# A linear-attention and gated-MLP block on one core: query blocks as seven products for eight, three PSUM banks a unit, and a computed order of the helpers

## The chip, the core and the metric

The kernel runs on one core of a Trainium2 chip. The core has five instruction queues that run at the same time and wait for each other by semaphores: TensorE (PE) for matmuls into PSUM, ScalarE (ACT), VectorE (DVE), GpSimd (POOL), and SyncE (SP), from which nearly all DMAs are issued here. PSUM is used as eight banks of 128 partitions by 512 float32. The metric is the device time of one execution in microseconds; it was run three times.

## The reference

```python
x = A_x                                   # [1, 2048, 640], bfloat16
xn = layernorm(x)                         # over the 640, eps 1e-5
q, k, v = split(xn @ wqkv)                # 32 heads of 20 columns each
phi = lambda t: where(t > 0, t + 1, exp(t)) + 1e-6
pq, pk = phi(q), phi(k)
kv = einsum("bhsd,bhse->bhde", pk, v)     # per head, 20 x 20
z = einsum("bhsd->bhd", pk)
num = einsum("bhqd,bhde->bhqe", pq, kv)
den = einsum("bhqd,bhd->bhq", pq, z)[..., None] + 1e-6
s = heads_to_columns(num / den) @ wo      # wo: [640, 640]
g = silu(relu(xn @ w1) @ w2)              # w1: [640, 1728], w2: [1728, 640]
return x + s * g
```

## The kernel before, in words

**Tiles.** The 2048 tokens are 16 tiles of 128 (`t`), or four chunks of 512 (`j`). The 640 columns are five blocks of 128 (`k`, `c`). The 1728 hidden columns are 13 blocks of 128 and one of 64 (`f`, 14 in all). Everything stays in SBUF after its load.

**The order of work.** A class `Sched` (L21) notes for each operation what it reads and writes, and puts in the semaphore waits that follow from it. It does not move anything: every engine executes its operations in the order in which the program text records them, so a helper on VectorE that stands early in the text and waits holds up all of VectorE's work recorded after it. The order is written out by hand, as lists of helpers beside each step of TensorE's work (L1100 to L1283 for the first half, L1560 to L1664 for the second).

**Stages.**
1. Layernorm statistics and normalisation of each tile (`bn` L467, `aggr` L472, `LN_norm` L497) on DVE, with the reciprocal root on POOL. The first four tiles are transposed by TensorE, the others by a transposing DMA on SP (`xnT_dma` L545).
2. Key tiles (`K_mm` L551): 10 matmuls of 320 columns into two banks, evacuated by ScalarE twice (`K_evac` L566: exp, relu, over both banks at once), and finished on DVE (`K_fin` L581) into `pk`. For tiles 8 to 11 one more matmul (`whole`, L562) writes the columns 320 to 511 of the first bank, so that a later instruction that adds to the whole bank finds it started.
3. Query blocks, transposed (`Q_mm` L607): for each chunk and each block of 128 columns, 5 matmuls of 512 columns, evacuated by ScalarE (exp, relu) and summed by DVE (`f_sum`) into `pqT`: 4 x 5 = 20 blocks.
4. Hidden blocks (`H_mm` L655, narrow block `H_half` L665), transposed, into `hT`. The tokens of the first chunk are not yet scaled when their hidden blocks of `HP` are made; `scale_rows` (L939) and `scale_bcast` (L942) bring the 512 row scales into every partition with four matmuls against the identity (L943) and a ScalarE copy, and `scale_h` (L948) multiplies them in.
5. The gram matrix `GT` of `xn` and `pk`, the sums `z` (`z_sum` L750, `z_col` L765), the denominators (`den` L782), their reciprocals on DVE (`den_rec` L794). SP stores the reciprocals to DRAM, each repeated for the 20 columns of its head (`den_store` L803), and loads them back in the layout of the queries (`load_recip` L811, one 640 KB transfer for a chunk each way). `divide` (L818) multiplies the queries by them on DVE.
6. `kv_group` (L1288) makes each head's 20 x 20 product from `GT`, masked by DVE, and `W_block` (L1317) its product with `wo`, so that the attention output is one product of the divided queries with the result, `wf`.
7. For pairs of tiles, `U_steps` (L1405) makes the gate (hidden times w2, evacuated with silu by `gate_q` L1352), and `O_steps` (L1477) the attention output, which DVE multiplies by the gate straight from PSUM (`s_out` L1540, `s_mult` L1515) and adds to x (`s_store` L1520), and SP stores, 160 KB a tile. The first pair of output tiles is made by plain tiles (`s_tile` L1535), the last pair too: `s_tile` of tile 14 and `s_last` (L1550), which takes tile 15 in three pieces of 224, 208 and 208 columns, with a product after each, the first piece added on POOL and stored on another queue.

**Seven products for eight.** Ten pairs of hidden blocks in the first half (`h_unit` L1002, two chunks of tokens by two blocks of columns), the gram matrix (`seven` L894), the gate and the middle output pairs use the Strassen-Winograd form: a 2 x 2 block product from seven products of sums and differences, which DVE prepares in SBUF (`h_S`, `h_T`, `g_S`, `g_T1` and so on, `u_S`, `u_T`, `o_S`, `o_T`). The 640 columns are split two blocks, two blocks, and a fifth that is left over and done plainly (`last`). A unit is seven steps, in the order s1, s5, s6, s2, s7, s3, s4, and takes four banks `bd`, `ba`, `bb`, `bc`:

```python
        def s7():
            mm(7, ba)
            cp(ps[bd], ("ps", bd), ba)
...
        def s4():
            mm(8, ba)
            dst = hT[:, i + 6, schunk(j1)]
            tt(dst, ps[ba], s5, ALU.add, [("ps", ba), skey], [("hT", j1, i + 6)])
...
            mm(4, bd)
```

That is: after product 1, ScalarE copies bank `ba` into `bb`, on which product 2 accumulates; product 5 goes to SBUF; after product 6, DVE adds `ba` and product 5 into `bc`, on which product 3 accumulates. After product 7 ScalarE copies `ba` into the fourth bank `bd`, on which product 4 accumulates, while `ba` takes product 8 (the left-over fifth block) and gives the fourth quarter.

Of the kernel before, what the change touches and what calls it, by code (L numbers as in the profile page):

```python
# [11 lines left out]
class _Res:  # L12
    __slots__ = ("w", "r", "nread")

    def __init__(self):
        self.w = None
        self.r = {}
        self.nread = 0


class Sched:  # L21

    def __init__(self, nc, n_dma_sems):
        self.nc = nc
        self.ops = {E: [] for E in ENGS}
        self.count = {E: 0 for E in CENGS}
        self.gseq = 0
        self.seq_at = {E: [] for E in CENGS}
        self.seq_at_dma = []
        self.vc = {E: {} for E in ENGS}  # L30
        self.vc_at = {E: [] for E in CENGS}
        self.vc_at_dma = []
        self.res = {}
        self.ndma = 0
        self.dma_sem_of = []
        self.dsem_count = [0] * n_dma_sems
        self.dsem_last_k = [None] * n_dma_sems
        self.n_dma_sems = n_dma_sems
        self.allow_unread = set()

# [18 lines left out]
    def _require(self, E, agents, waits):  # L59
        need_eng = {}  # L60
        need_dma = []
        for a in agents:
            if self._known(E, a):
                continue
            if a[0] == "D":
                if a not in need_dma:
                    need_dma.append(a)
            else:
                if need_eng.get(a[0], -1) < a[1]:
                    need_eng[a[0]] = a[1]  # L70
        items = [("E", Ep, idx, self.seq_at[Ep][idx]) for Ep, idx in need_eng.items()] + \
                [("D", a[1], None, self.seq_at_dma[a[1]]) for a in need_dma]
        items.sort(key=lambda x: -x[3])
        for kind, a1, a2, _sq in items:
            if kind == "E":
                Ep, idx = a1, a2
                if self._known(E, (Ep, idx)):
                    continue
                waits.append(("E", Ep, idx + 1))
                vc = self.vc[E]  # L80
                vc[Ep] = max(vc.get(Ep, 0), idx + 1)
                self._merge(E, self.vc_at[Ep][idx])
            else:
                k = a1
                if self._known(E, ("D", k)):
                    continue
                si, val = self.dma_sem_of[k]
                waits.append(("D", si, val))
                self.vc[E][("D", k)] = True
                self._merge(E, self.vc_at_dma[k])  # L90

    def _hazards(self, R, W):
        agents = []
        for key in R:
            st = self.res.get(key)
            if st is not None and st.w is not None:
                agents.append(st.w)
        for key in W:
            st = self.res.get(key)
            if st is not None:  # L100
                if st.w is not None:
                    agents.append(st.w)
                agents.extend(st.r.values())
        return agents

    def _update_res(self, agent, R, W):
        Rset = set(R)
        for key in R:
            st = self.res.get(key)
            if st is None:  # L110
                st = self.res[key] = _Res()
            rk = agent if agent[0] == "D" else agent[0]
            st.r[rk] = agent
            st.nread += 1
        for key in W:
            st = self.res.get(key)
            if st is None:
                st = self.res[key] = _Res()
            else:
                assert (st.w is None or st.nread > 0 or key in Rset or key in self.allow_unread  # L120
                        or (agent[0] == "PE" and st.w[0] == "PE")), (
                    "unread overwrite of %r by %r (prev writer %r)" % (key, agent, st.w))
            st.w = agent
            st.r = {}
            st.nread = 0

    def op(self, E, fn, R=(), W=(), extra=()):
        return self.group(E, [fn], R, W, extra)

    def group(self, E, fns, R=(), W=(), extra=()):  # L130
        assert E in CENGS
        waits = []
        agents = self._hazards(R, W) + list(extra)
        self._require(E, agents, waits)
        idx = self.count[E]
        self.count[E] += 1
        self.vc_at[E].append(dict(self.vc[E]))
        self.seq_at[E].append(self.gseq)
        self.gseq += 1
        self.ops[E].append(("op", waits, fns, idx))  # L140
        self._update_res((E, idx), R, W)
        return (E, idx)

    def dma(self, E, fn, sem_idx, R=(), W=(), extra=()):
        waits = []
        agents = self._hazards(R, W) + list(extra)
        prev = self.dsem_last_k[sem_idx]
        if prev is not None:
            agents.append(("D", prev))
# [14 lines left out]
    def wait_all_dma(self, E, sem_idxs):  # L164
        waits = []
        for si in sem_idxs:
            k = self.dsem_last_k[si]
            if k is None:
                continue
# [1527 lines left out]
```

## Time and profile before

| what | value |
|---|---|
| three runs | 208.28, 208.39, 210.0 us |
| median of them | 208.39 us |
| span of the profiled execution (the time that its page gives) | 207.0 us, 3745 instructions |
| granted TensorE clock, mean | 1.000 |
| DMA packets, moved | 32999, 24.74 MB, 119 GB/s mean |
| TensorE's first and last busy moment without a gap between | 4.49 and 204.51 us |

The answer on windows gives, in busy microseconds of TensorE, VectorE and ScalarE, by stage:

| us from the start | what is done there | PE | DVE | ACT |
|---|---|---|---|---|
| 4.49 to 23.61 | the first statistics, keys, hidden blocks of the first chunk | 19.09 | 16.84 | 14.84 |
| 23.61 to 63 | keys, queries, first four hidden units | 39.39 | 33.26 | 32.41 |
| 63 to 112 | six hidden units, queries, denominators | 49.0 | 40.19 | 36.33 |
| 112 to 146 | gram matrix, `kv_group`, `W_block`, first gate pair | 34.0 | 28.67 | 14.07 |
| 146 to 204.5 | gate and output pairs | 58.5 | 47.88 | 24.02 |

How to read the profile: times are microseconds from the span's first instruction. PE is TensorE's matmuls, PEld its weight loads. PEclk is the clock granted to TensorE, in tenths of full speed. In the chain of waits each line is a piece of the chain that ended last: its start, its length, engine, tile, line and number of instructions. A group's row has line, engine, operation, output and inputs with shapes and count, then busy time, mean nanoseconds of one, and the idle time before them with what ended it. A transfer's row has its tiles, queue, kind, count, KB of one and the median time from issue to landing.

### The profile page before, as it was taken

The page shows a single profiled execution, that of the slowest core. Times are in us where ns is not written, and L with a number is a line of the kernel's source. Part 1 is how long each engine was busy: PE and PEld are TensorE (multiplying, and loading weights), DVE is VectorE, ACT ScalarE, POOL GpSimd, SP SyncE. Part 2 cuts the span into 40 slices and gives each one's busy share as a digit, 9 for nine tenths or more (in the row PEclk, how much of TensorE's full clock was granted, in tenths as well). Part 3 has the DMA queues.
Part 4 walks back from the last instruction along what each step waited for, and adds up shares of the span by engine and source line. Part 5 has one row for each costly group of instructions (what it writes and reads, how often), then busy time and mean ns, then how long its engine had stood idle before and what let it go on. Part 6 is the DMA issues. An engine that isn't in the chain of part 4 may idle for free.

```text
span 207.0 us, 3745 instructions
## 1 busy us (share of the span) xinstructions
PE 203.6 (98%) x1400; PEld 126.3 (61%) x1400; DVE 169.7 (82%) x373; ACT 124.3 (60%) x251; POOL 18.0 (9%) x53
## 2 busy tenths in 40 slices
PE   8999999999999999999999999999999999999995
PEld 7755645545555444444456777777777777777773
DVE  4888997988969787686889669898888989897465
ACT  5598869888889987686563435462525354352531
POOL 3174032101330000000000000000000000000001
PEclk9999999999999999999999999999999999999999
DMA  6965999211037000302225999237931011010103
GB/s 194 331 190 117 255 203 275 42 32 29 6 63 198 25 3 0 127 0 57 74 63 114 251 357 384 90 108 234 371 129 63 3 63 46 21 63 0 63 5 127
DMA packets 32999, 24.74 MB, mean 119 GB/s; under 512 B 12757, under 2 KB 32981, under 8 KB 32981
## 3 DMA queue, kind: packets, MB, share of 16 engines
q1 hardware_dynamic: 31749, 23.13, 39.2%
q10 hardware_dynamic: 1232, 1.37, 1.9%
q8 instruction: 11, 0.18, 0.4%
q14 instruction: 7, 0.06, 0.1%
HBM read 15.81 MB, written 5.24 MB: 102 GB/s over the span
## 4 chain that ended last, share of the span: by engine, by line
PE 97%; DMA 1%; DVE 1%; issue 0%
PE psT L882 40%; PE psT L1036 19%; PE psT L556 11%; PE psT L609 11%; PE psT L658 6%; PE psT L1529 3%; PE psT L1580 2%; DMA reg<-in_A_x_dram 1%; PE psT L676 1%; PE psT L1320 1%; PE psT L530 1%; PE psT L1294 1%; PE psT L756 1%; PE psT L786 1%; PE psT L432 0%; DVE stats L469 0%
## 5 line engine op out<-in xcount | busy, mean ns | idle before, releaser
L882 PE MATMUL psT<-reg,regH 128*128 128x320 bf16 (+1 forms) x224 | 34.3, 299 | 0.0
L882 PE MATMUL psT<-reg 128*128 128x320 bf16 (+1 forms) x164 | 27.7, 299 | 0.0
L882 PEld LDWEIGHTS psT<-reg,regH 128*128 128x128 bf16 (+1 forms) x224 | 21.9, 98 | 8.6
L1354 ACT ACTIVATE wv_sb<-psT 128x320 bf16<-128x320 f32 x28 | 11.3, 436 | 25.2 <-PE psT L882 15.4
L609 PE MATMUL psT<-reg 128*128 128x512 bf16 x100 | 24.4, 379 | 0.0
L1036 PE MATMUL psT<-reg 128*128 128x512 bf16 x80 | 23.2, 379 | 0.0
L827 DVE TENSOR_TENSOR psT<-psT,reg 128x320 f32<-128x320 f32 x30 | 14.3, 493 | 9.3 <-PE psT L882 9.2
L889 ACT ACTIVATE psT<-psT 128x320 f32<-128x320 f32 x32 | 13.6, 426 | 11.2 <-PE psT L882 10.7
L882 PEld LDWEIGHTS psT<-reg 128*128 128x128 f16 (+1 forms) x164 | 16.0, 98 | 6.9 <-DVE regH L827 0.2
L889 ACT ACTIVATE reg<-psT 128x320 f32<-128x320 f32 (+1 forms) x24 | 10.4, 435 | 15.6 <-PE psT L882 13.6
L556 PE MATMUL psT<-reg 128*128 128x320 bf16 x120 | 17.9, 299 | 0.0
L1042 ACT ACTIVATE psT<-psT 128x512 f32<-128x512 f32 x20 | 11.9, 595 | 8.2 <-PE psT L1036 8.2
L569 ACT ACTIVATE regE<-psT 128x640 bf16<-128x640 f32 x24 | 15.6, 706 | 1.9 <-PE psT L556 1.2
L609 PEld LDWEIGHTS psT<-reg 128*128 128x128 bf16 x100 | 9.6, 98 | 11.6 <-issue 0.7
L1048 ACT ACTIVATE regH<-psT 128x512 bf16<-128x512 f32 (+1 forms) x24 | 14.5, 604 | 2.1 <-PE psT L1036 1.8
L556 PEld LDWEIGHTS psT<-reg 128*128 128x128 bf16 x120 | 11.5, 98 | 6.5 <-ACT regE L569 0.5
L469 DVE BATCH_NORM_STATS2 stats<-reg 128x6 f32<-128x320 bf16 x32 | 14.1, 475 | 1.3 <-DMA reg<-in_A_x_dram 1.3
L827 DVE TENSOR_TENSOR reg<-reg 128x1024 f16<-128x1024 bf16 (+6 forms) x17 | 13.5, 805 | 1.7 <-DMA reg<-in_B_w_dram 1.2
L882 PE MATMUL psT<-reg,pqT 128*128 128x320 bf16 (+1 forms) x72 | 14.7, 299 | 0.0
L1517 DVE TENSOR_TENSOR reg<-psT,wv_sb 128x640 bf16<-128x640 f32 (+2 forms) x16 | 11.8, 739 | 3.0 <-PE psT L882 1.8
L1036 PEld LDWEIGHTS psT<-reg 128*128 128x128 bf16 x80 | 7.7, 98 | 9.4 <-issue 0.4
L1522 POOL TENSOR_TENSOR reg<-reg 128x224 bf16<-128x224 bf16 x1 | 0.6, 607 | 144.0 <-DVE reg L1517 144.0
(143 smaller groups left out, 369.0 us busy)
## 6 DMA issues: line engine op xcount, KB each, us to landing
reg<-in_B_w_dram SPq DMA_DIRECT2D x12, 320.0 KB, 5.5
scr<-rden SPq DMA_DIRECT2D x4, 640.0 KB, 8.3
reg<-in_A_x_dram SPq DMA_DIRECT2D x4, 640.0 KB, 6.6
out_dram<-reg SPq DMA_DIRECT2D x15, 160.0 KB, 1.9
regE<-scr SPq DMA_DIRECT2D x3, 640.0 KB, 7.5
reg<-in_A_x_dram SPq DMA_DIRECT2D x4, 320.0 KB, 4.4
reg<-in_A_wo_dram SPq DMA_DIRECT2D x6, 160.0 KB, 3.3
reg<-in_A_x_dram SPq DMA_DIRECT2D x5, 160.0 KB, 5.5
```

What stands on the lines that cost most here:

```text
L469: sc.op("DVE", lambda eng: eng.bn_stats(stats[:, t, a, :], xv[:, HN * a:HN * (a + 1)]), R=[("xin", xs(t))], W=[("stats", t, a)])
L556: fns.append(lambda eng, a=a, k=k, lhs=lhs: eng.matmul(ps[b + a][:, 0:HN], lhsT=lhs, rhs=wk[:, k, HN * a:HN * (a + 1)], start=(k == 0), st ...
L569: sc.op("ACT", lambda eng: eng.activation(out=o_.rearrange("p (a n) -> p a n", a=2), in_=ps2(b, HN), func=func, scale=scale), R=[("ps", b) ...
L609: sc.group("PE", [(lambda eng, k=k: eng.matmul(ps[b], lhsT=wq[:, k, P * f:P * (f + 1)], rhs=xnT[:, j, k, :], start=(k == 0), stop=(k == C ...
L658: sc.group("PE", [(lambda eng, k=k: eng.matmul(ps[b], lhsT=w1_col(k, P * f, P), rhs=src[:, k, :], start=(k == 0), stop=(k == C - 1))) for ...
L827: sc.op("DVE", lambda eng: eng.tensor_tensor(out=out, in0=in0, in1=in1, op=op), R=R, W=W, extra=extra)
L882: sc.group("PE", [(lambda eng, k=k, lhs=lhs, rhs=rhs: eng.matmul(ps[b][:, 0:HN], lhsT=lhs, rhs=rhs, start=(start and k == 0), stop=(k == n ...
L889: sc.op("ACT", lambda eng: eng.activation(out=dst, in_=ps[b][:, 0:HN], func=ACTF.Copy), R=[("ps", b)], W=[dkey], extra=extra)
L1036: sc.group("PE", [(lambda eng, k=k, lhs=lhs, rhs=rhs: eng.matmul(ps[b], lhsT=lhs, rhs=rhs, start=(start and k == 0), stop=(k == n - 1), sk ...
L1042: sc.op("ACT", lambda eng: eng.activation(out=dst, in_=ps[b], func=ACTF.Copy), R=[("ps", b)], W=[dkey], extra=extra)
L1048: sc.op("ACT", lambda eng: eng.activation(out=dst, in_=ps[b], func=ACTF.Relu), R=[("ps", b)], W=[("hT", j, f)])
L1517: sc.op("DVE", lambda eng: eng.tensor_tensor(out=tmpo[:, os_, lo:hi].rearrange(shp, a=na), in0=src, in1=g_of(t)[0][:, lo:hi].rearrange(shp ...
```

## The change

**Query units.** Sixteen of the twenty query blocks (column blocks 0 to 3, four chunks) become four units of seven products (`p0`, `p1`, `q0`, `q1`); the fifth column block stays plain (`Q04` to `Q34`).

```diff
+    def q_unit(f, jp):
+        o = P * f
+        def done(half, j, src, skey):
+            both, sum_ = Q_evac(j, f + 2 * half, src, skey)
+            both()
+            pend.append(sum_)
+        def out22(j, b, s5, skey):
+            tt(s5, ps[b], s5, ALU.add, [("ps", b), skey], [skey])
+            done(1, j, s5, skey)
+        return unit(jp, lambda half, k: wq[:, k, o + 2 * P * half:o + 2 * P * half + P], [("wq",)],
...
+    def q_S(i):
+            tt(qSv[1], A21, A22, ALU.add, [("wq",)], [k(1)])
...
```

**Three banks.** All units lose the fourth bank and the copy into it. Product 8 is accumulated on product 7, the fourth quarter is read from there, and product 4 is accumulated on the same bank after it has been read; since the bank then holds product 8 too, product 4's left-over block takes the difference of the two operands (`x4d`, `oT[5]`), which DVE makes in SBUF.

```diff
         def s7():
             mm(7, ba)
-            cp(ps[bd], ("ps", bd), ba)
+            mm(8, ba)
+            out22(j1, ba, s5, skey)
...
         def s4():
-            mm(8, ba)
-            dst = hT[:, i + 6, schunk(j1)]
-            tt(dst, ps[ba], s5, ALU.add, [("ps", ba), skey], [("hT", j1, i + 6)])
...
-            mm(4, bd)
+            mm(4, ba)
...
-            4: (z([blk(1, 2), blk(1, 3)], tv(4)) + last(1, j0), w + [("hTs", 4)]),
+            4: (z([blk(1, 2), blk(1, 3)], tv(4)) + [(blk(1, 4), x4d[jp][:, ts])],
...
+            tt(x4d[jp], xnT[:, j0, 4, :], xnT[:, j1, 4, :], ALU.subtract, xall, [k(5)])
...
+        tt(oT[5], wf[:, 4, 0:HN], wf[:, 4, HN:D], ALU.subtract, wkeys, [("oT", 5)], ex)
```

The same is done in `seven` for the gram matrix, the gates and the outputs. The gate's fourth quarter is summed into the SBUF buffer of product 5 and not in place. The freed banks are handed out least recently used first (`take`) to the plain blocks. The first pair of output tiles becomes a unit too (`o0`).

**Key tiles 8 to 15 in halves.** Each half of 320 columns takes one bank and is evacuated by itself; the matmul that filled up the bank (L562) goes.

```diff
+    def K_half(t, a):
+        b = take(1)
+        K_mm(t, [b, b], halves=(a, ))
+        for func, slot, key in ((ACTF.Exp, 0, "ek_e"), (ACTF.Relu, 1, "ek_r")):
+            sc.op("ACT", lambda eng, func=func, slot=slot: eng.activation(
+                out=ek[:, eks(t), slot, HN * a:HN * (a + 1)], in_=ps[b][:, 0:HN], func=func),
...
```

**Row scales via DRAM.** The four matmuls and the copy go; SP stores 128 x 4 two-byte values to DRAM and loads them back as one row repeated in all partitions.

```diff
-    def scale_bcast(b):
-        sc.group("PE", [(lambda eng, t=t: eng.matmul(
...
+    def scale_out():
+        dma("SP", lambda eng: eng.dma_start(scs.rearrange("t p -> p t"), rsyH[:, :], allow_slow_non_contiguous=True),
+            R=[("rsyH",)], W=[("scs",)])
+    def scale_in():
+        src = scs.rearrange("t p -> (t p)").unsqueeze(0).to_broadcast([P, 4 * P])
+        dma("SP", lambda eng: eng.dma_start(rsyB, src), R=[("scs",)], W=[("rsyB",)])
```

**Output sums rounded by ScalarE.** ScalarE copies the output's sums from PSUM into a bfloat16 tile, and DVE multiplies that by the gate in SBUF. The three pieces of the last tile keep the product straight from PSUM.

```diff
     def s_out(t, src, keys):
...
-        s_mult(t, os_, 0, 0, D, ps2(b, HN), [("ps", b), ("ps", b + 1)], 2)
-        late.append(lambda: s_store(t, os_, (0, ), 0, D))
+        sc.op("ACT", lambda eng: eng.activation(
+            out=o_[:, 0:n].rearrange("p (a n) -> p a n", a=2) if n == D else o_[:, 0:n], in_=src, func=ACTF.Copy),
+            R=keys, W=both[0:len(keys)])
+        tt(o_, o_, g_of(t)[0], ALU.mult, both + [("g", gslot[t], 0), ("g", gslot[t], 1)], both)
+        s_store(t, os_, (0, 1), 0, D)
```

**The order.** A text lists TensorE's steps and the places of the helpers. The scheduler now records everything first; TensorE and SP keep the recorded order, and after the first part (`end_of_head`) ACT, DVE and POOL get an order computed from estimated costs: of the next 60 operations of an engine, the one that can start first, or one that is due earlier if it can start in time. The text's beginning and end:

```diff
+H14 H15 n8 T0 xa xb H111 n9 n10 xc ra H112 wb H110 Q04 a1.s5 a1.s1 n11 a0.s5 n12 Kb8 a0.s1 a1.s6 rb Ka8 SQ
...
+b4.s3 b4.s7 Q24 b4.s4 g0.s5 g0.s2 g0.s6 w2d dn g0.s7 c1
...
+o6.s1 o6.s5 st14 o6.s6 l0 o6.s2 o6.s3 o6.s7 l1 l2 o6.s4
```

The words are `H` hidden blocks, `Q` and `K` query and key blocks, `a` and `b` the hidden units, `p` and `q` the query units, `g` the gram units, `u` and `o` gate and output pairs, `n` normalisation, `ra` and `rb` the store and load of the row scales, `dn` the denominators, `do`, `rc` and `dv` the store, load and division by their reciprocals, `kv` and `W` the blocks of stage 6, `st14` the plain output tile 14 and `l0` to `l2` the three pieces of tile 15. So the middle output pairs' last unit, `o6` (tiles 12 and 13), now ends the program, after the three pieces of tile 15; before, tile 15's pieces ended it. The denominators (`dn`) stand after the first gram products; before, they stood in the fourth of the six second hidden units.

```diff
+    def place(self):
...
+                    can = [(max(free[E], ready[o.n]), o.late, o.n) for o in w[:self.LOOK] if not nleft[o.n]]
...
+                    est, late, n = min(can)
+                    c = recs[n]
+                    for e2, l2, n2 in can:
+                        if l2 < c.late and (e2 <= est or (e2 < est + c.occ and l2 < est + c.occ)):
+                            c, est2 = recs[n2], e2
...
+        return sorted(recs, key=lambda o: (o.start, o.n))
```

## The prediction, made before the changed kernel ran

> **What bounds the kernel now.** I read the busy shares first, then the chain that ended last, then its pieces in order of time.
>
> ```profile
> PE 203.6 (98%) x1400; PEld 126.3 (61%) x1400; DVE 169.7 (82%) x373; ACT 124.3 (60%) x251; POOL 18.0 (9%) x53
> ...
> PEclk9999999999999999999999999999999999999999
> ...
> PE 97%; DMA 1%; DVE 1%; issue 0%
> ```
> TensorE is the chain: 97% of it, at full granted clock in all forty slices. The pieces of that chain say that TensorE never stops between its first block at 4.49 us and 204.51 us, and what one matmul costs there.
>
> ```profile
> 25.77 0.22 PE psT L943 x4
> ...
> 34.97 0.08 PE psT L562
> ...
> 36.13 1.08 PE psT L609 x5
> ...
> 111.77 11.95 PE psT L882 x88
> ...
> 203.12 1.39 PE psT L1529 x15
> ...
> 204.53 0.38 DVE reg L1517
> ...
> 204.94 0.37 DVE reg L1522
> ```
> A matmul of 512 columns steps by 1.08/5 = 0.216 us, one of 320 columns by 11.95/88 = 0.136 us (the groups' means, 379 and 299 ns, are pipelined lengths). After the last matmul 2.5 us remain: a product, an add, a store. So only two things count: how many matmuls there are, and whether a new wait or a new tail takes back what fewer of them save. The rows for that are the evacuations (groups, shapes kept apart), then SP's own instructions in order of time, then the transfers with KB of one and median time to landing.
>
> ```profile
> L889 ACT ACTIVATE psT<-psT 128x320 f32<-128x320 f32 x32 | 13.6, 426 | 11.2 <-PE psT L882 10.7 <-DVE reg L827 0.5
> ...
> L1517 DVE TENSOR_TENSOR reg<-psT,wv_sb 128x640 bf16<-128x640 f32 x13 | 10.7, 822 | 2.8 <-PE psT L882 1.8 <-PE psT L1529 0.5
> ...
> L827 DVE TENSOR_TENSOR psT<-psT,wv_sb 128x512 f32<-128x512 f32 x10 | 7.0, 699 | 4.9 <-PE psT L1036 4.9
> ...
> L1522 DVE TENSOR_TENSOR reg<-reg 128x640 bf16<-128x640 bf16 x15 | 6.7, 484 | 0.0
> ```
> ```profile
> 109.76 1.34 SPq L806 DMA_DIRECT2D scr<-rden  x2
> ...
> 115.43 1.59 SPq L815 DMA_DIRECT2D reg<-scr  x1
> ```
> ```profile
> scr<-rden SPq DMA_DIRECT2D x4, 640.0 KB, 8.3
> ...
> out_dram<-reg SPq DMA_DIRECT2D x15, 160.0 KB, 1.9
> ...
> regE<-scr SPq DMA_DIRECT2D x3, 640.0 KB, 7.5
> ...
> reg<-scr SPq DMA_DIRECT2D x1, 640.0 KB, 7.3
> ...
> reg<-reg SPq DMA_TRANSPOSE x16, 2.7
> ...
> reg<-reg SPq DMA_DIRECT2D x1, 150.0 KB, 2.8
> ```
>
> **TensorE's work.** Sixteen of the twenty query blocks (5 matmuls of 512 each) become four units of 18: 80 - 72 = 8 fewer, 8 x 0.216 = 1.73 us. The broadcast of the row scales (L943) goes: 0.22. The four matmuls of L562 go: 4 x 0.08 = 0.32. The first pair of output tiles becomes a unit, 18 for 20 of 320 columns: 2 x 0.136 = 0.27. Every other unit keeps its count: the product that was added separately is now added after product 7, and product 4 takes the difference of the last operands instead. Sum **-2.54 us**, certain if TensorE stays fed, as this is the count of the built program.
>
> **The engines beside it.** DVE gains, by rows: query units 8 x 0.70 (sums out of PSUM), 4 x 0.42 (weight sums), 2 x 0.42 (differences of the last operand), 0.3 (the same for the output weights), the first output pair 2.2; it loses 15 x (0.82 - 0.48) as output products read SBUF: 5.6 + 1.7 + 0.8 + 0.3 + 2.2 - 5.1 = +5.5, to 175 us. ACT loses the copy of product 7 (10 x 0.60 and 16 x 0.43) and L946 (0.59), and gains 8 x 0.60 (query copies), 2.7 (K's 16 evacuations of 0.71 become 32 of 0.44), 8 x 0.70 and 7 x 0.44 (output sums), 0.9: +3.6, to 128 us. Neither becomes the bound in sum; what matters is where they are late. I walked the built order of each queue, with TensorE's steps added up from 23.61 us, where the order first differs, and the rows' durations.
>
> - First block, 23.61: it takes bank 0, which the ScalarE evacuation of K tile 6 frees some 0.07 us later; before, it took bank 4. **+0.07**.
> - 26 to 57 us: TensorE asks for the first units 2.6 us sooner (a query pair and a narrow block of 1.19 us moved back). DVE is the queue at risk: after the shared 26.97 us step its order gives the first token sum at 29.5 (needed 30.1), tile 9 normalised at 32.4. A transpose lands in 2.7: 35.2, needed 36.4; tile 10 38.5 against 39.5; tile 15, issued on SP at 47.9 behind two others of 1.26 each, 50.7 against 53.4. Covered by 1 us or more: 0.
> - The row scales go out as 512 elements of two bytes and come back spread over the rows, queued on SP at about 37.5 and 41.8, ahead of transposes 11 and 13. No row has such a write. Bounds: 1.9 to 2.8 us from the small copies of L1335 (the fence's last row), 10.4 from the slowest store of reciprocals. Transpose 11 is needed at 45.6 and the scaling at 50, so up to about 5 us nothing waits. I take 2.8 (nearest in bytes): 0; the upper end is a rival.
> - The denominators move 11 us later on TensorE (end 110.2 against 98.5), so the reciprocals end at 114.8 (0.7 + 4 x 0.82 + a 0.4 sum between). In the trace the first load ends 13.0 us after the first store's issue (115.43 + 7.3 - 109.76), with two weight loads in front that are now ahead of the stores: 114.8 + 13.0 = 127.8 at most, 125.8 by the shortest store and load (5.0 and 6.0 in the answers on those two tiles). DVE reaches the first division at 127.8. 0, with no room.
> - Seams: a unit now uses three banks, so product 4 waits for DVE to have read product 7. Tightest of the 512-column ones (unit a2): 1.08 us of other matmuls lie between, 0.05 + 0.70 + 0.06 is needed. Tightest of all, u3: 0.68 lie between product 1 and 2, ScalarE needs 0.05 + 0.43 + 0.06: 0.14 to spare, unless another 0.43 us evacuation is ahead of it. Below, nothing can be gained, as TensorE had no idle time; above, 31 units each once late by 0.1 would cost 3.1. I take 0, because the walk has each operation in its queue's order.
> - Tail. Before: 0.38 + 0.37 + store 1.7 = 2.5. After, the last matmuls belong to tile 13, whose sum ScalarE first copies (0.44), then DVE multiplies, does a waiting add of tile 15 and adds (0.40 + 0.29 + 0.48 from start to start), then 160 KB are stored (1.9): 0.1 + 0.44 + 1.17 + 1.9 = 3.6. **+1.1**. If the engines were a step sooner, +0.7; if the add waited behind both others in full, +1.4.
>
> Sum: -2.54 + 0.07 + 1.1 = **-1.4**: span 207.0 to 205.6. The median of the runs shown, 208.39, lies 1.4 above the span, so **207.0 us** (-0.7%).
>
> The granted clock was 1.00 in every stretch of before. The Trainium skill, "TensorE: Matmul & The Clock Gate", section "A second HAM failure mode: psum-queue depth-cycling", speaks against a change like this one: a kernel that cycles through PSUM banks with many short idles between its groups can fall back and forth between half and full clock. By this rule the sum would rest on a lower clock, not on counts; before, with eight banks in rotation and no idle, shows no sign of it.
>
> **Rivals.**
> 1. *The tail is hidden* or comes out at its short end, and everything stays fed: 208.39 - 2.54 + 0 to 0.4 = 205.9 to 206.3. For: the count is certain. Against: four operations in a row on two engines after the last matmul.
> 2. *Seam waits*: the slacks of 0.14 to 0.35 us, some twenty of them, are used up by my errors in start delays; 1.5 to 3.1 us in all: 208.5 to 210.1 (middle 209.0). Against: the trace shows ScalarE starting 0.04 us after the block that it reads.
> 3. *The first division blocks DVE*: with the medians 8.3 and 7.4 the row reciprocals land at 130.5, and behind the division stand the masked product that the W blocks need at 130.2 and the sums of unit u0. About 1.9 us: 208.9. For: DVE takes its queue in order.
> 4. *The other side, slower*: the two-byte write holds the queue. It decides from about 5 us on: at 10.4, transpose 11 lands near 50 instead of 42, and K half 11 (45.6) makes TensorE wait 4.5 us: 211.5. Against: 1 KB in all.
> 5. *The clock*: short waits at seams lower the granted clock. Half clock doubles a step of 0.216; over a tenth of TensorE's 178 us of remaining blocks that is +17.8: 225. Against: PEclk above.
> That the change does not do what it says is excluded for the count, not for its worth: 2 to 4 are that case.
>
> **How the numbers follow.** Forecast (206.3 to 208.0) 50%, rival 1 20%, rival 2 16%, rival 3 5%, rival 4 7%, rival 5 2%. A measurement of this kernel can tell about 1% from no change (206.3 and 210.5 are the marks). Faster by over 1%: rival 1 and the lowest edge of the forecast, 0.24. Slower by over 1%: rivals 4 and 5 and the top of rival 2, 0.14. Within: 0.62. The range 205.8 to 209.8 leaves out rivals 4 and 5 and the upper part of 2, about 0.15; the forecast's own range is 206.3 to 208.0.
>
> **What would show it.** TensorE's chain unbroken up to about 202.0 with 92 query matmuls: the count and the cover are right. A chain that passes through DVE or ACT between 30 and 200: rival 2, at the line it names. Idle of DVE before the division with a DMA as its releaser near 127: rival 3. TensorE waiting on a transpose near 45: rival 4. PEclk below 9: rival 5. After the last matmul 3.6 us: the tail. I am wrong if TensorE idles over 1 us in all, or the tail is under 3 us.

## The result, and the profile after

The changed kernel took 218.6 us (median of four runs, 217.59 to 220.15) against 209.19 for the kernel before in the same job: ratio 1.046, 95% interval 1.040 to 1.053. It is slower, and by more than the range allowed. Its profiled run is the longest of the four: 220.15 us, with a span of 218.8 and a mean granted clock of 0.972, where the other three have 0.984.

The page of the changed kernel, the same lines as before:

```profile
PE 202.6 (93%) x1371; PEld 124.5 (57%) x1382; DVE 168.0 (77%) x394; ACT 127.7 (58%) x265; POOL 18.3 (8%) x53
...
PE   8999999930799999999999999999999999999993
...
PEclk9999999995599999999999999999999999999998
...
PE 71%; DVE 12%; DMA 12%; issue 2%; POOL 2%; ACT 0%
```

TensorE has no more work than before, but the chain is not TensorE's alone now: a hole stands in slices 9 and 10, and behind it the granted clock is half. The chain of waits, cut to that place (start, length, what):

```profile
39.52 16.28 DMA reg<-reg
55.79 0.05 issue
55.84 1.51 PE psT L715 x5
57.35 1.71 PE psT L1198 x4
59.06 1.67 PE psT L818 x15
60.73 0.54 PE psT L1198 x2
61.27 0.68 PE psT L715 x5
```

The waits of TensorE (line, what it waited for: total, times, longest):

```profile
PE psT L715 <- DMA reg<-reg: 10.1, 1, 10.1
...
PE psT L800 <- ACT regE L725: 0.3, 1, 0.3
PE psT L766 <- DMA reg<-reg: 0.3, 1, 0.3
PE psT L1022 <- DVE psT L966: 0.2, 1, 0.2
```

One wait of 10.1 us, of a half key tile (L715) for a transpose. Five matmuls of 320 columns take 1.51 us right after it and 0.68 at 61.27: half clock. What SP had issued at that time:

```profile
37.38 0.58 SPq L538 DMA_DIRECT2D reg<-in_A_x_dram  x1
38.00 0.47 SPq L1080 DMA_DIRECT2D scs<-rsyH  x1
38.51 0.51 SPq L543 DMA_DIRECT2D reg<-in_B_w_dram  x1
39.52 2.54 SPq L704 DMA_TRANSPOSE reg<-reg  x2
54.75 0.34 SPq L1085 DMA_DIRECT2D wv_sb<-scs  x1
55.13 4.95 SPq L704 DMA_TRANSPOSE reg<-reg  x3
```

And how long the transfers issued from 37 to 44 us took to land (KB, last column: median us):

```profile
reg<-in_A_x_dram SPq DMA_DIRECT2D x1, 320.0 KB, 3.3
reg<-in_B_w_dram SPq DMA_DIRECT2D x1, 320.0 KB, 16.5
reg<-reg SPq DMA_TRANSPOSE x3, 16.3
scs<-rsyH SPq DMA_DIRECT2D x1, 1.0 KB, 16.7
```

The load ahead of the store of the row scales (L1080) landed in 3.3 us. The store itself, 1 KB, took 16.7, and what was issued behind it took as long: a load of w1 and transposes that need 2.6 elsewhere. The sizes fit: 10.1 us of wait, and from 55.84 to 61.27 TensorE took 5.43 us for blocks that take 3.28 in the first experiment below (45.98 to 49.26), 2.15 more. Together 12.3 us; without them the profiled run would end near 206.5.

The evacuations and reciprocals, the rows that answer to those of before (shapes kept apart, then transfers):

```profile
L1811 DVE TENSOR_TENSOR reg<-reg 128x640 bf16<-128x640 bf16 x15 | 7.3, 503 | 0.1
...
L966 DVE TENSOR_TENSOR psT<-psT,wv_sb 128x512 f32<-128x512 f32 x10 | 6.9, 694 | 1.3 <-PE psT L1198 1.2
...
L966 DVE TENSOR_TENSOR reg<-reg,wv_sb 128x640 bf16<-128x640 bf16 x13 | 6.1, 486 | 3.0 <-ACT reg L1833 2.9
...
L1833 ACT ACTIVATE reg<-psT 128x640 bf16<-128x640 f32 x8 | 5.6, 701 | 3.8 <-PE psT L1022 3.0 <-PE psT L1818 0.8
```
```profile
scr<-rden SPq DMA_DIRECT2D x4, 640.0 KB, 5.7
...
regE<-scr SPq DMA_DIRECT2D x3, 640.0 KB, 4.9
```

These are as costed: a product from SBUF 0.486 us for 0.822, a sum of 512 columns 0.694 for 0.699, ScalarE's copy 0.70.

### The profile page after: what moved, and what is told of

It reads as the page before. It is cut to its first block, busy times and chain, and to the rows that moved or that the text cites. A ratio compares the mean times of both kernels' runs of the same rounds, so it can differ in the third digit from the quotient of the medians.

```text
span 218.8 us, 3714 instructions
## 1 busy us (share of the span) xinstructions
PE 202.6 (93%) x1371; PEld 124.5 (57%) x1382; DVE 168.0 (77%) x394; ACT 127.7 (58%) x265; POOL 18.3 (8%) x53
## 4 chain that ended last, share of the span: by engine, by line
PE 71%; DVE 12%; DMA 12%; issue 2%; POOL 2%; ACT 0%
PE psT L1022 35%; PE psT L1198 22%; DMA reg<-reg 10%; PE psT L715 5%; DVE stats L636 3%; PE psT L1490 2%; DVE reg L966 2%; PE psT L766 2%; POOL rsy L644 1%; DVE reg L655 1%; PE psT L818 1%; DMA reg<-in_A_x_dram 1%; PE psT L800 1%; DVE regH L966 1%; DVE psT L966 1%
## 5 line engine op out<-in xcount | busy, mean ns | idle before, releaser
L1198 PE MATMUL psT<-reg 128*128 128x512 bf16 (+1 forms) x123 | 35.7, 383 | 0.2
L715 PE MATMUL psT<-reg 128*128 128x320 bf16 x120 | 19.8, 306 | 10.3 <-DMA reg<-reg 10.1
L966 DVE TENSOR_TENSOR reg<-reg 128x1024 f16<-128x1024 bf16 (+8 forms) x27 | 18.3, 692 | 5.8 <-DMA reg<-reg 1.6
L715 PEld LDWEIGHTS psT<-reg 128*128 128x128 bf16 x120 | 11.7, 99 | 17.9 <-DMA reg<-reg 10.4
L1198 PEld LDWEIGHTS psT<-reg 128*128 128x128 bf16 (+1 forms) x130 | 12.6, 99 | 14.4 <-issue 1.2
L1476 ACT ACTIVATE regE<-psT 128x320 bf16<-128x320 f32 x32 | 12.5, 453 | 12.5 <-PE psT L715 12.3
L1248 ACT ACTIVATE regH<-psT 128x512 bf16<-128x512 f32 (+1 forms) x24 | 14.6, 607 | 4.8 <-PE psT L1198 4.6
L966 DVE TENSOR_TENSOR psT<-psT,reg 128x320 f32<-128x320 f32 (+1 forms) x20 | 10.6, 534 | 5.4 <-PE psT L1022 5.3
L777 ACT ACTIVATE regE<-psT 128x512 bf16<-128x512 f32 x16 | 9.4, 604 | 5.9 <-PE psT L1198 3.0
L966 DVE TENSOR_TENSOR reg<-psT,reg 128x320 bf16<-128x320 f32 (+2 forms) x18 | 9.0, 509 | 4.7 <-PE psT L1022 3.7
L1833 ACT ACTIVATE reg<-psT 128x640 bf16<-128x640 f32 (+1 forms) x15 | 8.3, 576 | 4.9 <-PE psT L1022 4.1
L644 POOL TENSOR_TENSOR rsy<-rsv,mhalf 128x1 f32<-128x1 f32 x16 | 10.0, 630 | 1.2
```

The lines of the kernel that those rows point to most:

```text
L644: sc.op("POOL", lambda eng: eng.tensor_tensor(out=rsy[:, t:t + 1], in0=rsv[:, t:t + 1], in1=mhalf[:, :], op=ALU.pow), R=[("rsv", t), ("mha ...
L715: fns.append(lambda eng, a=a, k=k, lhs=lhs: eng.matmul(ps[bk[a]][:, 0:HN], lhsT=lhs, rhs=wk[:, k, HN * a:HN * (a + 1)], start=(k == 0), st ...
L777: exps.append(sc.op("ACT", lambda eng: eng.activation(out=e_, in_=src, func=ACTF.Exp), R=[key], W=[("er_e", es)]))
L966: sc.op("DVE", lambda eng: eng.tensor_tensor(out=out, in0=in0, in1=in1, op=op), R=R, W=W, extra=extra)
L1198: sc.group("PE", [(lambda eng, k=k, lhs=lhs, rhs=rhs: eng.matmul(ps[b][:, 0:nn], lhsT=lhs if tile is None else rhs, rhs=rhs if tile is Non ...
L1248: sc.op("ACT", lambda eng: eng.activation(out=dst, in_=ps[b], func=ACTF.Relu), R=[("ps", b)], W=[("hT", j, f)], extra=ex)
```

## The experiments

The theory after the result: the store of 512 two-byte elements holds what is queued behind it, and that alone makes the kernel slower. The rivals: the new order makes transposes late in any case; SP, which waits 12.7 us at the dependent load, is what holds them; the seams of the units cost several us.

**1. Row scales by matmul again** (everything else of the change stays).

```diff
-        dma("SP", lambda eng: eng.dma_start(scs.rearrange("t p -> p t"), rsyH[:, :], ...
-        dma("SP", lambda eng: eng.dma_start(rsyB, src), R=[("scs",)], W=[("rsyB",)])
+        b = take()
+        sc.group("PE", [... ps[b][:, P * t:P * (t + 1)], lhsT=rsyH[:, t:t + 1].to_broadcast([P, P]), rhs=ident ...
+        sc.op("ACT", ... out=rsyB, in_=ps[b], func=ACTF.Copy ...
```

> The changed kernel, but with the row scales spread by four matmuls and a ScalarE copy as before, in place of the store to DRAM and the load. Theory (the store of 512 two-byte elements, 16.7 us from issue to landing, holds the transposes issued behind it, TensorE waits 10.1 us for one and then runs some 4 us at half clock): the wait and the half clock go, four matmuls of 0.05 us come back: 218.6 - 10.1 - 2.1 + 0.2 = 206.6, and 206.0 to 208.0 allowed; no idle of TensorE over 0.5 us, clock 1.00. Rival A (the computed order lets VectorE normalise the tiles too late, so that the transposes are late in any case): above 212, a wait of TensorE on a transpose remains near 45 us. Rival B (the three-bank seams cost several us by themselves): 209 to 212 with no large wait.

Measured: 208.8 us (207.75 to 209.23), ratio 1.000 (0.998 to 1.002), above the 206.0 to 208.0 that the theory allowed; no listed wait for a transpose; clock 1.00 up to the last matmul (the mean of 0.998 comes from what follows it, 0.86 in 203.2 to 206.9 us):

```profile
PE psT L598 <- PEq L1913: 0.8, 1, 0.8
PE psT L714 <- ACT regE L1477: 0.3, 1, 0.3
```

The theory's wait is gone, and with it the loss against the kernel before. The forecast's gain is not there either: that is taken up in the point-by-point section.

**2. The dependent load later.** SP does not stand at the load any more before the transposes of tiles 13 to 15.

```diff
- ... a1.s6 rb Ka8 ...      ... n15 p1.s6 ...
+ ... a1.s6 Ka8 ...         ... n15 rb p1.s6 ...
```

> The changed kernel, but SP issues the load of the row scales after the last transpose and not before the transposes of tiles 13 to 15, so that SP waits for the store's landing with nothing behind it. Theory (the store itself holds what is queued behind it): the transposes issued at 39.5 us land near 55 us all the same, TensorE's wait of 10 us stays: 217 to 220. Rival (SP, which stands 12.7 us at the load waiting for the store, is what holds the transposes): the wait goes, 206 to 209.

Measured: 219.44 us (one run); the store landed in 15.9 us; TensorE waited 9.1 us for a transpose. It is the store and not SP's wait.

**3. Eight-byte pieces.** The same 1 KB, laid out by partition.

```diff
-    scs = nc.dram_tensor("scs", [4, P], f16, kind="Internal").ap()
+    scs = nc.dram_tensor("scs", [P, 4], f16, kind="Internal").ap()
-  eng.dma_start(scs.rearrange("t p -> p t"), rsyH[:, :], allow_slow_non_contiguous=True)
+  eng.dma_start(scs, rsyH[:, :])
-        tt(hTh[:, f, 0:512], hT[:, f, 0:512], rsyB, ALU.mult, ...
+        tt(v(hTh[:, f, 0:512]), v(hT[:, f, 0:512]), rsyB.rearrange("q (p t) -> q t p", t=4), ALU.mult, ...
```

> The changed kernel, but the row scales lie in DRAM by partition, so that the store writes 128 pieces of 8 bytes in place of 512 of 2 (VectorE reads the row back with a stride in its products). Theory, with a price by the piece: a quarter of 16.7 is 4.2 us to landing, which the slack of about 5 us covers: 206.0 to 208.5. Rival, a price that a small write to DRAM has whatever its pieces: landing stays above 12 us, 215 to 219.

Measured: 208.11 us (207.48 to 209.34), ratio 0.997 (0.9945 to 1.000). Transfers from 36 to 60 us:

```profile
reg<-reg SPq DMA_TRANSPOSE x6, 2.6
scs<-rsyH SPq DMA_DIRECT2D x1, 1.0 KB, 3.7
```

3.7 us for 16.7, and the transposes behind it are at 2.6 again.

**4. The store alone added to the kernel before.**

```diff
-    first = [[(N, 10)], [(N, 11)], ...
+    first = [[(scale_out, ), (N, 10)], [(N, 11)], ...
```

> The kernel before, with only one thing added: SP stores the 512 row scales as two-byte elements to DRAM, ahead of the transpose of tile 10; nothing reads them. Theory: that transpose, issued at about 38.5 us, lands some 16 us later, near 54, and the key tile that TensorE takes at 46.26 waits about 8 us, with 2 us more at half clock after it: 217 to 220. Rival (the store harms only together with the load that waits for it, or with the new order): 208 to 210.

Measured: 214.24 us (one run) against 208.59. The store took 16.1 us to land, and TensorE's one new wait is this:

```profile
PE psT L557 <- DMA reg<-reg: 4.0, 1, 4.0
```

The mechanism holds without anything else of the change. The size was off because SP reached the store at 33.8 us, not 38.5: the transpose issued at 37.77 landed 12.3 us later, at 50.1, for a key tile due at 46.26. From 50.23 TensorE took 5.44 us for blocks that took 3.60 before (46.42 to 50.02), 1.84 more; with the 4.0 of wait that is 5.8, and the spans differ by 5.7 (212.7 and 207.0).

**5. Half as many elements.**

```diff
-  dma_start(scs.rearrange("t p -> p t"), rsyH[:, :], ...
+  dma_start(scs[0:2, :].rearrange("t p -> p t"), rsyH[:, 0:2], ...
```

> The changed kernel, but the store writes 256 of the 512 two-byte row scales and the load repeats them (so tokens 256 to 511 get the scales of tokens 0 to 255; everything else is as it was). Theory, a price by the piece: 128 pieces of 8 bytes landed in 3.9 us and 512 pieces of 2 in 16.7, that is (16.7 - 3.9) / 384 = 0.033 us a piece, so 256 land in 8.1 us; the transposes behind come 8.6 us sooner than in the changed kernel, TensorE waits 1 to 2 us instead of 10.1 and keeps its clock: 207.5 to 210.0. Rival, a size under which all such stores cost the same: landing above 12 us, 215 to 219.

Measured: 217.31 us (one run); landing 15.1 us; wait 8.3 us. The price by the piece falls: half the pieces cost nearly the same. (The 3.9 us in the expectation is the landing of the load; the store of eight-byte pieces took 3.7.)

**6. Small stores by themselves.** Five stores at 65 us in the kernel before, each waiting for the one before.

```diff
+    probe("pa512x2", [4, P], tp, 4)
+    probe("pb256x2", [2, P], tp, 2)
+    probe("pc128x2", [1, P], tp, 1)
+    probe("pd128x8", [P, 4], lambda d: d, 4)
+    probe("pe512x2wide", [4, P, 32], lambda d: d[:, :, 0].rearrange("t p -> p t"), 4)
```

> The kernel before with five small stores added on SP after the loads of wo, near 65 us, where its DMA engines are idle, each waiting for the landing of the one before; nothing reads them (its time is not the question). Landing of 512 pieces of 2 bytes, 256 of 2, 128 of 2, 128 of 8 bytes, and 512 of 2 bytes at 64 bytes from each other. Theory 1 (the store of two-byte pieces is slow by itself, as 16.7 and 15.1 us with 512 and 256 suggest): over 12 us for the first two, under 5 for 128 of 8 bytes; if neighbours in one line of DRAM are the reason, the spaced one is under 8. Theory 2 (it is slow through the transposes that run beside it): all land in under 6 us.

Since each waits for the landing of the one before, the starts give the times (SP's queue):

```profile
65.84 0.43 SPq L1193 DMA_DIRECT2D pa512x<-rsyH  x1
79.78 0.38 SPq L1193 DMA_DIRECT2D pb256x<-rsyH  x1
94.33 0.33 SPq L1193 DMA_DIRECT2D pc128x<-rsyH  x1
110.03 0.33 SPq L1193 DMA_DIRECT2D pd128x<-rsyH  x1
113.00 0.37 SPq L1193 DMA_DIRECT2D pe512x2wide<-rsyH  x1
```

and the landing of the last (transfers from 60 to 116 us):

```profile
pe512x2wide<-rsyH SPq DMA_DIRECT2D x1, 1.0 KB, 2.5
```

512, 256 and 128 adjacent pieces of two bytes take 13.9, 14.6 and 15.7 us; 128 pieces of eight bytes 3.0; 512 pieces of two bytes at 64 bytes from each other 2.5, each measured once. So it is neither the number of pieces nor the bytes nor the company of transposes: two-byte pieces from different partitions that lie side by side in DRAM are slow. Nor is it the sending that lasts: for the second store the DMA view of this run has 272 packets from 79.7 to 82.5 us and none from 82.5 to 94.3, so by these records the pieces are on their way within 3 us, and the rest of the 14.6 passes until the landing is reported. Why, no run here shows.

**7. The store on ScalarE's queue.**

```diff
-        dma("SP", lambda eng: eng.dma_start(scs.rearrange("t p -> p t") ...
+        dma("ACT", lambda eng: eng.dma_start(scs.rearrange("t p -> p t") ...
```

> The changed kernel, with the store of the 512 two-byte row scales issued from ScalarE's queue and not SP's. Theory 1 (what is queued behind the store on SP's own queue waits for it): the transposes of tiles 11 and 12 land in some 3 us, TensorE's 10 us wait goes; SP still stands at the load until the store has landed, so the transposes of tiles 13 to 15 come at 55 to 60, just about when TensorE needs them: 207.5 to 210. Theory 2 (the store occupies the DMA engines themselves, whatever queue it came from): the wait stays, 215 to 220.

Measured: 222.47 us (one run). The computed order issued the store at 23.6 us instead of 38.0, so its time compares badly, but the question is answered. The transfers issued from 22 to 45 us:

```profile
reg<-in_A_x_dram SPq DMA_DIRECT2D x2, 320.0 KB, 13.4
reg<-reg SPq DMA_TRANSPOSE x5, 14.7
scs<-rsyH ACTq DMA_DIRECT2D x1, 1.0 KB, 17.2
```

Transposes and loads of SP's own queue wait for a store of another queue (TensorE waited 12.2 us, at the first query block). Another queue is no way round it.

**8 and 9. The two-byte store where no transpose is behind it.** First the store after the last transpose and the products with the scales some steps later; then the products also 60 us later.

```diff
- ... xc ra H112 ...   ... rb Ka8 ...   ... p1.s7 ZS wa Kb11 ...     ... p0.s4 b0.s6 ...
+ ... xc H112 ...      ... Ka8 ...      ... p1.s7 wa ra Kb11 ...     ... p0.s4 rb ZS b0.s6 ...     (8)
+ ... xc H112 ...      ... Ka8 ...      ... p1.s7 wa ra Kb11 ...     ... p0.s4 rb b0.s6 ... w2b ZS GS1 ...     (9)
```

> The changed kernel with the two-byte store as it is, but issued after the transpose of tile 15 and the last load of w1, and the load and the products with the scales (which only the gate products need, 80 us later) some us behind it. Theory (it is harmful only through what is queued behind it): no wait of TensorE for a transpose, clock 1.00, 207.5 to 208.8, ratio 0.995 to 1.001. Rival (two-byte stores harm wherever they stand): above 211.

Measured: ratio 1.050 (1.047 to 1.053), median of four runs 219.34 us: a miss, and an instructive one. No transpose was late. But VectorE takes its order as it stands:

```profile
71.16 0.43 DVE L966 TENSOR_TENSOR regH<-regH,wv_sb 128x512 f16<-128x512 bf16 x1 [10.65 <-DMA wv_sb<-scs]
```

It stood 10.65 us at the first product with the scales, because the computed order had costed the store and the load at about 2 us each; TensorE waited 8.9 us for VectorE.

> As the run with the late store, but the five products with the row scales stand 60 us later in the order, ahead of the first gate sums that need them. In that run VectorE stood 10.7 us at the first of them for the load that follows the store, and TensorE waited 8.9 us for VectorE. Theory (the slow store harms only through what waits behind it): no wait of TensorE above 0.9 us, clock 1.00, 207.8 to 209.2, ratio 0.996 to 1.003. Rival (a two-byte store slows the kernel wherever it is): above 211.

Measured: ratio 1.001 (0.998 to 1.004). So the slow store costs next to nothing where nothing that is needed soon waits for it, be it in the DMA queues or on VectorE. One thing did not come out as expected: the profiled run (210.55 us) has a wait of 1.3 us for VectorE at 67 us, above the 0.9 allowed. Just before it ScalarE and VectorE stood for 3.5 and 3.0 us, while the store was still in flight (SP issued the load that waits for it at 68.56). What held them the profile does not show.

**10. The four query units undone** (on the kernel of 3): each of their seven-step units becomes four plain blocks, and their weight sums go.

```diff
- ... a0.s3 p1.s5 Ka10 p1.s1 a0.s2 a0.s7 p1.s2 n15 p1.s6 Kb9 ...
+ ... a0.s3 Ka10 Q01 a0.s2 a0.s7 Q11 n15 Kb9 ...
```

> The changed kernel with the store in pieces of eight bytes, and its four query units undone: all twenty query blocks are plain again, 80 matmuls for 72, without the units' copies, sums and weight sums. Theory by the count: 8 x 0.216 = 1.73 us more than 208.11, so 209.8, ratio 1.003 to 1.007. Rival (the seams of the units, with a matmul's start later by some hundredths each, and the extra helpers take back most of it): 208.0 to 208.9, ratio 0.997 to 1.001.

Measured: 212.61 us, ratio 1.019 (1.015 to 1.022), further than either side said. By the count 1.73 us of it are matmuls. TensorE's listed waits (its start left out) are 4.0 us against 1.0 in the kernel of 3. Of these 3.0 more, 1.2 lie at the first query block (1.9 us for a transpose, against 0.7), ahead of everything that the edit changes; the same block waited 0.2 to 1.2 us in the runs of 11 to 13. Most of the others are waits in the new order. The sum, 1.73 + 3.0, meets what was measured within 0.4 us (4.5 between the medians, 5.1 between the spans), which fits the units' count; that plain blocks would cost 4 us in a well-fitted order is not shown.

**11. Products straight from PSUM** (on the kernel of 3).

```diff
-        sc.op("ACT", ... out=o_[:, 0:n] ... in_=src, func=ACTF.Copy ...
-        tt(o_, o_, g_of(t)[0], ALU.mult, ...
+            tt(o_ ..., src, g_of(t)[0] ..., ALU.mult, ...
```

> The changed kernel with the store in pieces of eight bytes, and the output sums multiplied by VectorE straight from PSUM, as before the change, in place of ScalarE's rounded copy. Theory (ScalarE's copy serves VectorE's load, and costs only in the tail): VectorE has some 5 us more in a stage in which it is busy 3/4 of the time, which hides; the tail is 0.4 us shorter: 207.7, ratio 0.993 to 0.997. Rival (the copy was needed: VectorE is late at the seams without it): 208.5 to 211, ratio 0.999 to 1.01.

Measured: 209.86 us, ratio 1.005 (1.002 to 1.008). VectorE rises from 168.9 to 172.6 us busy; its last add ends 1.65 us after TensorE's last matmul in place of 1.8, but TensorE's end comes 1.4 us later. By the ratios, 1.005 against 0.997, ScalarE's copy pays. The profiles do not bear all of that out: 0.95 of the 1.4 us is there by 69 us (0.44 before the first query block and 0.5 at it), ahead of every output product. From there to the end of the span it is 0.7 us; how much of that is the copy's is not shown.

**12 and 13. Another end** (on the kernel of 3): two pieces of tile 15 behind product 4; then the last unit ahead of tile 14.

```diff
- o6.s1 o6.s5 st14 o6.s6 l0 o6.s2 o6.s3 o6.s7 l1 l2 o6.s4
+ o6.s1 o6.s5 st14 o6.s6 o6.s2 o6.s3 o6.s7 l0 o6.s4 l1 l2      (12)
+ o6.s1 o6.s5 o6.s6 o6.s2 o6.s7 o6.s3 o6.s4 st14 l0 l1 l2      (13)
```

> The changed kernel with the store in pieces of eight bytes (which ran at 208.11, ratio 0.997 to the kernel before), and the program's end reordered: the second and third piece of tile 15 stand behind product 4 of the last unit, so that the last matmuls are a piece's, read from PSUM by VectorE directly, as before the change. Theory (the tail after the last matmul is 3.8 us against 2.5 before, because ScalarE's copy, two products and two adds follow it): about 1.1 us less, 207.0, ratio 0.990 to 0.994. Rival (VectorE's queue sets the end whatever stands last): no change, ratio 0.996 to 0.999.

> The changed kernel with the store in pieces of eight bytes, and its end in another order: the last unit (tiles 12 and 13) first, then tile 14 plainly and the three pieces of tile 15, as the kernel before ends. In the run with two pieces behind product 4, TensorE waited 0.2 and 0.4 us for VectorE, and VectorE still had 1.6 us of work after the last matmul. Theory (VectorE's queue of sums, products and adds sets the end, so what counts is how much of it comes after the last matmuls): tile 13's product and add lie beside tile 14's matmuls now, 0.5 to 1 us less than 208.3: 207.3 to 207.8, ratio 0.993 to 0.997. Rival (the same work ends at the same time in any order): 0.997 to 1.000.

Measured: ratios 1.000 (0.997 to 1.002) and 1.003 (1.000 to 1.005). No gain in the times. Product 4 accumulates on the bank that VectorE must have read, and with fewer other matmuls between TensorE waits for VectorE: 0.2 us in 12, and at another place a weight load 0.4. Counted from 48 us on and against the profile of 3, TensorE's last matmul ends 0.14 us later in 12 and 0.6 in 13, and what follows it is 0.46 and 0.6 us shorter: in 13 the one takes back the other, and the 0.3 us that 12 would gain do not show in its times.

**14. Two repairs** (on the kernel of 3): a load of x behind two transposes, one add of the end on GpSimd.

```diff
- H14 H15 n8 T0 xa xb H111 n9 n10 xc ra ...
+ H14 H15 n8 T0 xa H111 n9 n10 xb xc ra ...
-        s_store(t, os_, (0, 1), 0, D)
+        s_store(t, os_, (0, 1), 0, D, "POOL" if t == 14 else "DVE")
```

> The changed kernel with the store in pieces of eight bytes and two small repairs: one load of x is issued after the transposes of tiles 9 and 10 instead of ahead of them, and GpSimd makes the last add of tile 14. Theory (the first query block's wait of 0.2 to 0.7 us for a transpose comes from loads beside it, and the end from VectorE's queue, in which that add takes 0.4): 0.5 to 1.0 us less than the 208.1 to 208.5 of that kernel, 207.3 to 207.9, ratio 0.992 to 0.997. Rival (other small waits take their place): ratio 0.997 to 1.001.

Measured: 210.99 us, ratio 1.011 (1.008 to 1.015): worse. The first query block still waited 0.7 us, other waits for VectorE came to 1.5 us, and at the end:

```profile
203.19 2.13 POOL L1812 TENSOR_TENSOR reg<-reg 128x224 bf16<-128x224 bf16 x2 [153.69 <-DVE reg L1807]
...
204.35 1.33 DVE L966 TENSOR_TENSOR reg<-reg,wv_sb 128x640 bf16<-128x640 bf16 x1
```

GpSimd's two adds took 2.13 us (one was of 640 columns), and VectorE's product beside them 1.33 instead of 0.486. The add was taken off VectorE and cost it more than the 0.4 us that it saved; from TensorE's last matmul to the end it is 4.5 us in place of 3.8.

So the fastest version is that of experiment 3, 0.3% below the kernel before; that is at the edge of what can be told from no change.

## Why the prediction was wrong, point by point

**The step that failed** is "I take 2.8 (nearest in bytes): 0" for the row scales via DRAM. The store alone took 16.7 us. It was recognised as the case on the other side (rival 4: the two-byte write holds the queue, decides from about 5 us on, 211.5), at the right place and by the right mechanism, with a chance of 0.07. Two things about it were wrong. The upper bound, 10.4 us, was the slowest store of 640 KB; that no row of the trace had pieces of two bytes was said, and then a bound was taken from rows that differ in just that. And the price left out what follows the wait: half clock for 2.15 us. With the measured wait of 10.1 us in place of the 4.5 that follow from 10.4, and the half clock, the rival's sum is 205.6 + 10.1 + 2.15 = 217.9 of span; the profile has 218.8.

The Trainium skill, "DMA: Bandwidth & Descriptors", section "Rules for kernel authors", says that a strided last dimension becomes one descriptor per element and should be rearranged to be contiguous. Experiment 3 is that advice, and it worked: 3.7 us for 16.7. As an explanation it falls short here: 512 spaced two-byte pieces are as many elements and took 2.5 us, 128 adjacent ones 15.7. The same page, section "Back-pressure in remote DMA", says of transfers between cores that stalled writes hold an engine's other queues too; experiment 7 shows the like within one core, 14.7 us for transposes of the other queue.

**The count** was right: 1400 TensorE instructions before, 1382 on the page of experiment 3, with eight query matmuls fewer and no L562. Experiment 10 fits 1.73 us for the units.

**TensorE stays fed** was not right even without the store. In experiment 1 TensorE needs 180.2 us from its first block behind the part that is the same in both, at 22.89 us, to the end of its last matmul (203.11); before, 181.06 (23.45 to 204.51). That is 0.84 less, where 2.54 less 0.22 were forecast. Of the 1.5 between, 0.7 are idle time: the windows give 9.65 and 9.86 busy of 10 us around 29 and 149 us (before, 10.00 and 10.00), and 0.22 more before product 4 in the end. Another 0.6 are longer steps: 52.72 / 242 = 0.2179 us in the units of 512 columns for 39.01 / 180 = 0.2167, and 83.86 / 615 = 0.1364 for 83.13 / 612 = 0.1358, so 252 x 0.0012 + 630 x 0.0005. The other 0.2 is not located. The 0.22 and the 0.14 around 149 us are waits for VectorE at a unit's product, as rival 2 has it, and 0.25 around 29 us is a wait of a key half for ScalarE; that the longer steps come from the seams too is not shown. The walk also missed a wait: TensorE asks for the first query block at 28.5 us, before at 30.4, and its transpose then comes late, by 0.1 us in experiment 1, 0.3 in the changed kernel and 0.7 in experiment 3.

**The tail** was +1.1 and is +1.3: the last matmuls of experiment 1, and what comes after them until the span's end at 206.9:

```profile
202.53 0.58 PE L1021 MATMUL psT<-reg,pqT 128*128 128x320 f16 x3
202.79 0.64 DVE L1807 TENSOR_TENSOR reg<-psT,wv_sb 128x208 bf16<-128x208 f32 x2
203.15 0.44 ACT L1834 ACTIVATE reg<-psT 128x320 bf16<-128x320 f32 x1 [1.16 <-PE psT L1021]
203.36 0.47 DVE L1812 TENSOR_TENSOR reg<-reg 128x640 bf16<-128x640 bf16 x1
203.76 0.48 DVE L965 TENSOR_TENSOR reg<-reg,wv_sb 128x640 bf16<-128x640 bf16 x1
204.16 0.76 DVE L1812 TENSOR_TENSOR reg<-reg 128x416 bf16<-128x416 bf16 x2
```

ScalarE's copy, the product and the adds follow each other as predicted; 206.9 - 203.1 = 3.8 for 3.6 (2.5 before). The sum without the store is -0.84 + 1.25 = +0.4, and the medians differ by +0.2 (208.8 for 208.59). The spans differ by -0.1, because in the two profiles the part that is the same in both took 22.89 and 23.45 us. With the four matmuls back the forecast would be 207.2; the 1.6 us to 208.8 are the 1.5 that TensorE did not save and 0.15 of the tail.

**VectorE's load** was forecast at 175 us and is 168.0 (167.8 in experiment 1), less than the 169.7 before. The forecast added the rows' durations to the page's busy time. By the rows, count times mean, VectorE's operations do add up to 4.5 us more (192.2 for 187.7), but where two overlap the busy time counts them once. Nothing hung on it.

**The denominators** (rival 3) did no harm: VectorE's longest wait for a load of reciprocals was 0.7 us, at a later division (1.1 in experiment 1), and the stores and loads took 5.7 and 4.9 us for 8.3 and 7.5. The end of the reciprocals in the prediction, 114.8, is 0.2 more than its terms add up to.

**The clock** (rival 5) fell, but not by short waits: in experiments 1 and 3, with all the seams, it was 1.00 from 20 us to the last matmul, and their means of 0.998 and 0.999 come from what follows that (0.86 and 0.92 granted there). It fell after about 4 us of the long idle and came back about 4 us after work resumed (0.94 in 48 to 50 us, 0.50 in 50 to 60, 1.00 from 60 on). In experiment 4 a wait of 4.0 us was enough: 0.94 in 50 to 51 us, 0.50 to 54, 0.85 in 54 to 55, which is half clock for 3.4 us. By the Trainium skill, "TensorE: Matmul & The Clock Gate", Part 1, idle or work over a window of about 3.4 us flips the clock between half and full; the trace agrees. The Trainium skill's rule on PSUM cycling, cited in the prediction as what would speak against the change, shows no sign here.

**The chances**: slower by over 1% had 0.14, and the one case with a new kind of operation in a queue that the bound engine waits on should have had more. The loss came from 1 KB, put at nothing in bytes, on the one resource whose price no row gave.

## What to carry to other kernels

An operation whose kind the profile has never shown is not bounded by rows that are nearest in bytes: ask what is behind it on every queue and engine, work out the delay from which it decides, and if a short run can measure it alone, do so before trusting it. Do not write adjacent two-byte pieces from many partitions to DRAM: eight bytes from each partition, or a gap between the pieces, took a fifth of the time here. On an engine at 97% with no idle, 0.84 of the 2.32 us taken from the count were kept here; the rest went in small waits and in steps longer by half a per cent, and the tail grew by 1.25, more than was kept. Count the tail as a stage.

## What the runs showed of the hardware that was not expected

- A store of 128 to 512 adjacent two-byte pieces takes 13.9 to 15.7 us alone, whatever their number; 128 pieces of eight bytes 3.0, 512 of two bytes 64 bytes apart 2.5. The packets of the one of 256 pieces fall in its first 3 us (272 from 79.7 to 82.5, none up to 94.3).
- Such a store delays transposes and loads of its own queue (16.3 and 16.5 us for 2.6 and 3.3) and of the other queue (14.7 us).
- A multiplication of 128 x 640 on VectorE took 1.33 us for 0.486 while GpSimd added tiles in SBUF (experiment 14). In experiment 1 an add of 128 x 640 took 0.78 for 0.50 beside GpSimd's add of 224 columns.
